# A multi-query attention and MLP block: one term of a software exp moved to GpSimd, GpSimd tied to a port order, and another rule for filling TensorE

## The chip, the cores and the metric

The kernel runs on one core of a Trainium2 chip. The metric is the device time of one execution in microseconds (us); the span in a profile is about 1.7 us shorter. Each run also reports the mean clock that TensorE was granted, as a share of full speed. That number matters more here than usual: the same program can take 809 or 880 us, and the clock tells which of the two it was. A run is called slow in the results when it lies over 1.5% above the fastest run of the same kernel. I compare runs by their clock.

## The reference, cut to what matters

```python
# S = 2048 tokens, D = 640, H = 32 heads of Dh = 20, one shared k and v; F = 1536
q = (xn @ wq) -> [H, S, Dh];  k = xn @ wk;  v = xn @ wv
scores = einsum("bhqd,bkd->bhqk", q, k) * Dh ** -0.5
o = einsum("bhqk,bkd->bhqd", softmax(scores), v)
out = x + o @ wo + (relu(xn @ w1 + b1) ** 2) @ w2 + b2      # xn = layernorm(x)
```

The scores are 32 x 2048 x 2048 numbers, and each needs an exp. The kernel cuts them into 2048 tiles of 128 keys x 512 queries. Everything else is small beside that. Below, "scores" is the first product, and "PV" the second, of the exps with v.

## The kernel before

The kernel is a Python list scheduler. It holds a model of the engines (a duration for each operation, semaphore latencies), places every operation in the model's time, and emits one fixed order for each engine. So the number of exp steps, of tiles given to VectorE and of filling matmuls is fixed when the kernel is built. When I speak below of "the schedule's own time" I mean this layout; it says what was planned, and nothing about how long the chip takes.

A block is 4 heads x 512 queries (32 blocks); for each of 16 key tiles it needs four score tiles. Most score tiles go to ScalarE, two to a step. Four at a time ("a set") go to VectorE, which makes an approximate exp out of bits. These are the parts that the change touches:

```python
ACT_BANKS = ((0, 1), (2, 3))      # PSUM banks of the tiles for ScalarE
DBANKS = (4, 5, 7); DPAIR = (4, 5); PVB = 6      # banks for VectorE's tiles; the PV accumulator
UTIL = 0.66
...
# an exp step on ScalarE: two tiles, 1024 columns
e.activation(out=PT[:, s0:s0 + n, :], in_=ps[:, b0:b0 + n, :], func=AF.Exp, bias=-EXP_SHIFT, scale=SCALE)
...
# a set on VectorE: scores to 16-bit patterns L (D1), two maskings (W, U), two products (T1, T2)
d1.parts = [lambda e: e.tensor_scalar(out=lbuf[a][:, cs].bitcast(U16), in0=src, scalar1=XA, scalar2=XB, op0=ALU.mult, op1=ALU.add)]
W:  tensor_scalar(W, L, 0xFF80, 124,    bitwise_and, bitwise_or)          # VectorE, 2048 columns
U:  tensor_scalar(UU, L, 0x7F, 0x3F80,  bitwise_and, bitwise_or)          # VectorE
T1: tensor_tensor(T, L, UU, mult)                                          # VectorE
T2: tensor_tensor(T, T, UU, mult)      # every other set on GpSimd in two pieces, else VectorE
# exp = L*v + W*(0.5 v) + T*(0.164 v): three PV products for each set, in that order
...
def commit(op):                         # the model lets VectorE and GpSimd run "lock" operations only in turn
    s = start_of(op, op.ready())        # (they share an SBUF port); on the chip nothing enforces it
    ...
def pe_use(t):                          # busy TIME of TensorE in the last 3.4 us
    ...
# before an operation that TensorE would have to wait for:
while pick[0] > free["PE"] + 0.1 + ... and pe_use(...) < UTIL:
    in_pv = pv_blk[0] < NBLK and pv_blk[0] in pv_begun
    fb = [x for x in DBANKS if ...free...]
    if not in_pv and not fb: break
    # a "fill": four matmuls with zero weights into the PV bank or a free score bank
    f_ = Op("fill", "PE", 0.215, [mm(ps[32*jj:32*jj+32, bk, :], zeros32[:, :], kT[:, 0:512], ...) for jj in range(4)], ...)
```

The score matmuls have only 20 rows (Dh) of the array's 128 and the full 128 columns. PV, the MLP and the output use all 128 rows, in four column strips at once.

The softmax here doesn't subtract the row's maximum and nothing guards it: scores larger than these inputs give would overflow.

## Time and profile before

| what | value | view |
|---|---|---|
| runs at the start | 879.42, 824.65, 808.65 us | the runs |
| profiled run | span 868.8 us, clock 0.916 | the cores |
| exp steps on ScalarE | 828 (1656 tiles); 98 sets (392 tiles) on VectorE | groups of instructions |
| ScalarE, 100 to 400 us | busy 298.34 of 300 us, 323 steps, so 0.924 us a step | windows |
| the same, 600 to 720 us | busy 76.83 of 120 us, 75 steps, clock 0.50 | windows |

These are lines of the page of the kernel before. The first is the span, the second the busy time of each engine; in the two others each digit is a fortieth of the span (21.7 us), in tenths.

```profile
span 868.8 us, 22692 instructions
PE 850.7 (98%) x10258; PEld 244.7 (28%) x10258; DVE 683.1 (79%) x998; ACT 786.4 (91%) x845; POOL 319.3 (37%) x211
...
ACT  6799999999999999999899999996666668999995
PEclk9999999999999999999799999995555557999999
```

TensorE's 98% is no use as a measure: ends of matmuls are modelled in the profile, and its row stays at 9 even where the clock halves. ScalarE's row is the one to read. After the start-up it stands at 9 (once at 8) except where the clock row falls to 5, and there it falls to 6. So two things bound this kernel: ScalarE's exp steps, and a TensorE clock that sometimes halves, so that the score matmuls come too late for ScalarE.

The windows view of the kernel before shows the two states side by side (columns: the stretch, its length, busy us and instructions of each engine, clock, DMA share, GB/s):

```profile
core 0: us, PE busy (x) PEld busy (x) DVE busy (x) ACT busy (x) POOL busy (x), PEclk, DMA share, GB/s
100.00:400.00 300.00, 295.29 (x3684) 83.24 (x3685) 261.04 (x363) 298.34 (x323) 123.70 (x76) 1.00 0.02 6
600.00:720.00 120.00, 120.00 (x937) 25.39 (x935) 61.06 (x86) 76.83 (x75) 26.49 (x14) 0.50 0.01 4
```

Next, groups of instructions of the kernel before by line and shape: count, then busy us and the mean ns of one, then the idle time before them and what ended it. L634 is the exp step, L768 the conversion to bits (single and two-bank), L774 W (one of its two groups), L776 U, L778 T1, L785 and L783 the second product T2 on VectorE and on GpSimd.

```profile
L634 ACT ACTIVATE PT<-ps 128x1024 bf16<-128x1024 f32 x828 | 778.2, 1059 | 65.1 <-PE ps L291 62.5
L768 DVE TENSOR_SCALAR x_sb<-ps 128x512 uint16<-128x512 f32 x326 | 218.6, 682 | 107.5 <-PE ps L291 107.0
L783 POOL TENSOR_TENSOR dextra<-dextra 128x1024 bf16<-128x1024 bf16 x98 | 207.5, 2130 | 337.8 <-DVE dextra L778 337.8
L778 DVE TENSOR_TENSOR dextra<-x_sb,dextra 128x2048 bf16<-128x2048 bf16 x98 | 118.5, 1209 | 0.0
L776 DVE TENSOR_SCALAR dextra<-x_sb 128x2048 uint16<-128x2048 uint16 x98 | 75.8, 774 | 0.0
L785 DVE TENSOR_TENSOR dextra<-dextra 128x2048 bf16<-128x2048 bf16 x49 | 59.3, 1211 | 0.0
L774 DVE TENSOR_SCALAR x_sb<-x_sb 128x2048 uint16<-128x2048 uint16 x66 | 45.4, 688 | 0.1
L768 DVE TENSOR_SCALAR x_sb<-ps 128x1024 uint16<-128x1024 f32 x33 | 40.2, 1219 | 18.3 <-PE ps L291 18.2
```

Added up, one set costs VectorE 2.64 (conversion, 258.8/98) + 0.69 (W) + 0.77 (U) + 1.21 (T1) + 0.61 (T2 on half of the sets) = 5.92 us. It takes two steps, 1.85 us, off ScalarE.

**Where the clock halves.** "TensorE: Matmul & The Clock Gate" (the Trainium skill), Part 1, states that a monitor looks at TensorE's activity in free-running windows of 3413 ns and grants half or full clock (1.2 or 2.4 GHz). The trace agrees on window and states: the two low stretches last 10.24 us and 136.5 us, which are 3 and 40 windows, and the clock is 0.5 in them. This is the timeline of TensorE just before the first of them, which begins at 415.5 us (columns: start, length, then what ran):

```profile
411.64 0.62 PE L291 MATMUL ps<-kT,zeros 128*32 128x512 bf16 x8
412.24 0.39 PE L291 MATMUL ps<-qT,kT 20*128 20x512 bf16 x3
412.56 0.40 PE L291 MATMUL ps<-PT,vx 128*32 128x512 bf16 x4
413.15 0.39 PE L291 MATMUL ps<-qT,kT 20*128 20x512 bf16 x2 [0.20 <-ACT PT L634]
414.07 0.39 PE L291 MATMUL ps<-qT,kT 20*128 20x512 bf16 x2 [0.53 <-ACT PT L634]
414.39 0.40 PE L291 MATMUL ps<-PT,vx 128*32 128x512 bf16 x4
```

It is the border between two blocks. The one PV bank is being read out, no fill (`kT,zeros`) is placed, and for 1.4 us (412.97 to 414.39) only score matmuls run, which use 20 rows of 128.

I therefore weighted every matmul of the trace by its **array share**: rows/128 times columns/128, for as long as its moving columns take at the granted clock. (At 2.4 GHz 512 columns are 0.213 us; groups of four strips start 0.22 us apart in the full-clock timeline, for instance 414.39, 414.61, 414.83.) Averaged over the chip's own windows, whose phase is known from the drops (the moments at which the clock falls to half), the two windows before the drops have 0.351 and 0.374. No other window at full clock between 45 us and the last matmul is as low (the next holds 0.378); the mean is about 0.55. This weighting is mine, worked out from the trace; it is no view of the profile.

**The shared port.** "SBUF — State Buffer", "Who interferes with whom", states that VectorE in its two-port modes and GpSimd share a pair of SBUF ports and that whoever comes first blocks the other for the whole instruction. The trace agrees: here W (L774), 0.69 us otherwise, took 1.33 us because GpSimd's square (L457) had begun 0.27 us earlier, and it ended 0.55 us after the square did, a little less than a whole W.

```profile
117.97 1.04 POOL L457 TENSOR_TENSOR big<-hT_tmp 128x512 bf16<-128x512 bf16 x1
118.24 1.33 DVE L774 TENSOR_SCALAR dextra<-x_sb 128x2048 uint16<-128x2048 uint16 x1
```

Over the whole kernel before, such stretching was small: about 9 us of VectorE, nearly all in U (98 times 0.77 - 0.69).

### The profile page before, as it was taken

Reading aid. Unit: us, or ns where it says so; the run is one execution under the profiler, and the core shown is the slowest. Engines: PE = TensorE matmul, PEld = TensorE weight load, DVE = VectorE, ACT = ScalarE, POOL = GpSimd, SP = SyncE. Lnnn points to the kernel's source line nnn. Section 1 sums busy time; section 2 is a strip of 40 time slices with the busy share of each in tenths; the row PEclk is TensorE's granted clock in tenths of the full one; section 3 lists DMA queues with packets and bytes.
Section 4 is the critical chain, followed back from the end, with each engine's and each line's share of the span. In section 5 each row is a group of like instructions: output and inputs, shape, how many; then the busy total and the mean of one; then the engine's idle time right before and its main releaser. Section 6 shows DMA issues by size and latency. Waiting matters only on the chain.

```text
span 868.8 us, 22692 instructions
## 1 busy us (share of the span) xinstructions
PE 850.7 (98%) x10258; PEld 244.7 (28%) x10258; DVE 683.1 (79%) x998; ACT 786.4 (91%) x845; POOL 319.3 (37%) x211
## 2 busy tenths in 40 slices
PE   8999999999999999999999999999999999999997
PEld 3322222222233233222233333221112222322333
DVE  7688888989888888889779887886455457988893
ACT  6799999999999999999899999996666668999995
POOL 5244355452423242534433424444122212342421
PEclk9999999999999999999799999995555557999999
DMA  9300000000000000000000000000000000000000
GB/s 323 90 2 2 2 2 2 2 2 2 2 17 2 17 17 2 16 2 2 2 17 2 17 17 17 2 2 1 1 1 2 16 2 16 17 17 2 2 2 32
DMA packets 11715, 14.94 MB, mean 17 GB/s; under 512 B 2017, under 2 KB 10978, under 8 KB 11618
## 3 DMA queue, kind: packets, MB, share of 16 engines
q1 hardware_dynamic: 10306, 13.44, 4.9%
q8 instruction: 80, 1.31, 0.6%
q10 hardware_dynamic: 1312, 0.05, 0.1%
q14 instruction: 17, 0.14, 0.1%
HBM read 10.87 MB, written 2.62 MB: 16 GB/s over the span
## 4 chain that ended last, share of the span: by engine, by line
PE 62%; ACT 36%; DMA 1%; DVE 1%; issue 0%; SPq 0%; DVEq 0%
PE ps L291 62%; ACT PT L634 35%; DMA x_sb<-in_A_x_dram 1%; DVE out_sb L980 0%; PE ps L403 0%; ACT PT L327 0%; ACT PT L324 0%; DVE Tn L680 0%; ACT xnT L376 0%; SPq L214 0%; DVE T L682 0%; ACT qT L431 0%; PE ps L902 0%; DVE w_sb L529 0%; DVEq L130 0%
## 5 line engine op out<-in xcount | busy, mean ns | idle before, releaser
L634 ACT ACTIVATE PT<-ps 128x1024 bf16<-128x1024 f32 x828 | 778.2, 1059 | 65.1 <-PE ps L291 62.5
L291 PE MATMUL ps<-qT,kT 20*128 20x512 bf16 x2048 | 367.9, 409 | 10.6 <-ACT PT L634 8.2
L768 DVE TENSOR_SCALAR x_sb<-ps 128x512 uint16<-128x512 f32 (+1 forms) x359 | 258.2, 731 | 125.8 <-PE ps L291 125.2
L783 POOL TENSOR_TENSOR dextra<-dextra 128x1024 bf16<-128x1024 bf16 x98 | 207.5, 2130 | 337.8 <-DVE dextra L778 337.8
L291 PEld LDWEIGHTS ps<-qT,kT 20*128 20x128 bf16 x2048 | 82.8, 92 | 340.8 <-ACT PT L634 253.7
L291 PE MATMUL ps<-PT,vx 128*32 128x512 bf16 x1656 | 175.0, 413 | 0.5 <-ACT PT L634 0.5
L778 DVE TENSOR_TENSOR dextra<-x_sb,dextra 128x2048 bf16<-128x2048 bf16 x98 | 118.5, 1209 | 0.0
L291 PE MATMUL ps<-w_sb,big 128*32 128x320 bf16 x1536 | 88.6, 322 | 0.0
L682 POOL TENSOR_TENSOR T<-Tn 128x512 bf16<-128x512 f32 x31 | 43.3, 1397 | 116.7 <-DVE Tn L681 116.7
L291 PE MATMUL ps<-xnT,w_sb 128*32 128x512 bf16 x960 | 81.1, 397 | 0.0
L776 DVE TENSOR_SCALAR dextra<-x_sb 128x2048 uint16<-128x2048 uint16 x98 | 75.8, 774 | 0.0
L291 PE MATMUL ps<-kT,zeros 128*32 128x512 bf16 x816 | 75.3, 414 | 0.0
L291 PEld LDWEIGHTS ps<-PT,vx 128*32 128x32 bf16 x1656 | 42.8, 94 | 108.4 <-issue 103.4
L457 POOL TENSOR_TENSOR big<-hT_tmp 128x512 bf16<-128x512 bf16 x48 | 54.2, 1134 | 51.0 <-DVE hT_tmp L449 50.9
L291 PE MATMUL ps<-wo_pad,OTn 128*32 128x320 bf16 x1024 | 60.6, 322 | 0.8 <-DVE w_sb L529 0.8
L785 DVE TENSOR_TENSOR dextra<-dextra 128x2048 bf16<-128x2048 bf16 x49 | 59.3, 1211 | 0.0
L291 PE MATMUL ps<-xnT,wq_sb 128*20 128x512 bf16 x640 | 57.8, 417 | 0.0
L291 PEld LDWEIGHTS ps<-w_sb,big 128*32 128x32 bf16 x1536 | 36.7, 99 | 33.4 <-issue 21.2
L774 DVE TENSOR_SCALAR x_sb<-x_sb 128x2048 uint16<-128x2048 uint16 x66 | 45.4, 688 | 0.1
L291 PE MATMUL ps<-x_sb,vx 128*32 128x512 bf16 x392 | 40.9, 407 | 0.2 <-DVE Tn L680 0.2
L291 PE MATMUL ps<-dextra,vxc 128*32 128x512 bf16 x392 | 41.1, 409 | 0.0
L680 DVE STREAM_TRANSPOSE Tn<-ps 128x512 f32<-128x512 f32 x32 | 22.9, 714 | 23.2 <-PE ps L291 23.1
(70 smaller groups left out, 386.3 us busy)
## 6 DMA issues: line engine op xcount, KB each, us to landing
w_sb<-in_B_w_dram SPq DMA_DIRECT2D x2, 1920.0 KB, 16.4
xr<-in_A_x_dram SPq DMA_DIRECT2D x16, 160.0 KB, 2.3
out_dram<-out_sb SPq DMA_DIRECT2D x16, 160.0 KB, 1.8
x_sb<-in_A_x_dram SPq DMA_DIRECT2D x3, 640.0 KB, 8.7
wq_sb<-in_A_wq_dram SPq DMA_DIRECT2D x1, 800.0 KB, 7.4
wo_pad<-in_A_wo_dram SPq DMA_DIRECT2D x4, 200.0 KB
x_sb<-in_A_x_dram SPq DMA_DIRECT2D x2, 320.0 KB, 3.8
wk_c<-in_A_wk_dram ACTq DMA_DIRECT2D x1, 25.0 KB, 3.5
```

What stands on the lines that cost most here:

```text
L291: return lambda e: e.matmul(out_, l, r, start=start, stop=stop, tile_position=tp)
L457: sq = q(Op(f"SQ{qc}_{f}", "POOL", 1.2, [lambda e: e.tensor_tensor(out=h2T[:, qc % 2, f, :], in0=hT_tmp[:, k % 2, :], in1=hT_tmp[:, k % 2, ...
L634: return Op(f"ACT{st_['j']}", "ACT", 0.064 + 0.4267 * n, [lambda e: e.activation(out=PT[:, s0:s0 + n, :], in_=ps[:, b0:b0 + n, :], func=AF ...
L680: tn = Op(f"TN{b}", "DVE", 0.72, [lambda e: e.transpose(out=Tn[:, a, :], in_=ps[:, PVB, :])], [lastpv, tm_op.get(b - 2)])
L682: tm = Op(f"TM{b}", *(("POOL", 1.3) if b in TM_POOL else ("DVE", 0.69)), [lambda e: e.tensor_tensor(out=T2[:, a, :].rearrange("p (c d) -> ...
L768: d1.parts = [lambda e: e.tensor_scalar(out=lbuf[a][:, cs].bitcast(U16), in0=src, scalar1=XA, scalar2=XB, op0=ALU.mult, op1=ALU.add)]
L774: s["wop"] = [dv(f"W{n}", 0.74, lambda e: e.tensor_scalar(out=W.bitcast(U16), in0=L.bitcast(U16), scalar1=0xFF80, scalar2=124, op0=ALU.bit ...
L776: s["uop"] = dv(f"U{n}", 0.74, lambda e: e.tensor_scalar(out=UU.bitcast(U16), in0=L.bitcast(U16), scalar1=0x7F, scalar2=0x3F80, op0=ALU.bi ...
L778: s["t1"] = [dv(f"T1_{n}", 1.235, lambda e: e.tensor_tensor(out=T, in0=L, in1=UU, op=ALU.mult), [s["uop"]] + ([("pv", old, 2)] if old else ...
L783: s["t2"].append(dv(f"T2_{n}", 2.15, lambda e, ks=ks: e.tensor_tensor(out=T[:, ks], in0=T[:, ks], in1=UU[:, ks], op=ALU.mult), s["t1"], 4, ...
L785: s["t2"].append(dv(f"T2_{n}", 1.235, lambda e: e.tensor_tensor(out=T, in0=T, in1=UU, op=ALU.mult), s["t1"], P_T))
```

## The change

Its intent, in four parts:

1. The approximate exp is made of other terms: 2**e (W), L*u (T) and a shifted pattern S, the bits of L plus 32. S replaces the second product. GpSimd makes it for every set, straight from L, in two pieces.
2. GpSimd waits for the VectorE operation that precedes it in the model's port order.
3. VectorE's conversions may take any two neighbouring banks (before: banks 4 and 5 only); the PV bank moves to 7.
4. Fills are asked for by array share (0.54 over 3.4 us and 0.4 over 1.7 us) instead of by busy time (0.66), and may be added onto a score tile that waits for ScalarE, when there is no other bank.

The diff holds one thing more: the three PV products of a set may now be issued in any order, each as soon as its term is ready.

The core of the diff (cut; the renaming of buffers and the bookkeeping of PV terms are left out):

```diff
-DBANKS = (4, 5, 7); DPAIR = (4, 5); PVB = 6
+DBANKS = (4, 5, 6); PVBS = (7,); MERGE = 2
-T2POOL = (0, 1)
+SPOOL = (1,)
-UTIL = 0.66
+UTIL = ((3.4, 0.54), (1.7, 0.4))
...
+    def cells(self):
+        if self.name.startswith("QK"):
+            return 0.156 * len(self.parts) * self.dur
+        if self.name.startswith("DQK"):
+            return 0.156 * 0.215
+        return self.dur * (0.625 if self.name.startswith(("QT", "KT")) else 1.0)
...
             if op.lock:
                 lock_free[0] = op.fin
+                if op.eng == "DVE":
+                    lock_dve[0] = op
+                elif lock_dve[0] is not None:
+                    op.deps.append(lock_dve[0])
...
-  W: (L & 0xFF80) | 124 ; U: (L & 0x7F) | 0x3F80 ; T1: T = L*UU
-  T2: T = T*UU on GpSimd (two pieces, 2.15 in the model) for every other set, else on VectorE
+  W:  X & 0xFF80       ; U: T = (X & 0x7F) | 0x3F80 ; T = X*T
+  S on GpSimd, two pieces, 1.06 in the model:
+     e.tensor_scalar(out=M[:, ks].bitcast(U16), in0=X[:, ks].bitcast(U16),
+                     scalar1=float(XS), scalar2=1.0, op0=ALU.add, op1=ALU.mult)
...
+  sa = steps[act_next] if ... and steps[act_next]["qk"].fin is not None else None
+  if not in_pv and not fb and sa is not None and free["PE"] + 0.1 + 0.215 + 0.2 <= free["ACT"]:
+      bk = sa["banks"][len(sa["tiles"]) - 1]
+      f_ = Op("fill", ... mm(ps[32*jj:32*jj+32, bk, :], zeros32[:, :], kT[:, 0:512], False, ...) ...)
+      sa["fill"].append(f_)          # and the exp step then waits for the fill
```

## The prediction

> **What bounds the kernel.** ScalarE's exp, 828 steps of two score tiles. In the windows view, 100 to 400 us, ScalarE is busy 298.3 of 300 us with 323 steps, 0.924 us a step; VectorE 87%. The other 392 of 2048 tiles (98 sets of four) go to VectorE's approximate exp. Each set moved there takes two steps, 1.85 us, off ScalarE.
>
> The second bound is the clock. The profiled run (868.8 us) has the TensorE clock at 0.5 from 415 to 426 us and from 589 to 726 us. From 600 to 720 us there are 75 steps instead of about 130. All lost steps come to about 60 us, so an unthrottled run should be near 809 us; the fastest run is 808.65. So 824.65 and 879.42 are throttle. "TensorE: Matmul & The Clock Gate", Part 1, says that activity in a window of 3413 ns sets a half or full clock; this trace agrees: both low stretches are whole multiples (10.24 and 136.5 us). Weighting each matmul in the trace by the share of the array it uses, the windows just before the drops have 0.35 and 0.37, the lowest since the start-up; the mean is about 0.55. By busy time alone, start-up windows were lower without a drop. Score matmuls use 20 of 128 rows, so they count little: that is why filling by busy time missed them.
>
> **What the change does, per set on VectorE** (durations by line and form): scores to bits 2.6 us, W 0.69, U 0.69 (mean 0.77 with stretching), T1 1.21, and T2 1.21 on half the sets: 5.9 us. T2 leaves VectorE. More one-instruction pairs of score banks are allowed: 1.22 instead of twice 0.68. New: about 5.2 us, 12% less. GpSimd's share is two pieces a set. Its two-input multiply (2.13 us for 1024) can't price a one-input pass; memsets of 512 and 5120 columns (0.53, 4.36 us) give 0.85 us per 1024 plus some start, so an estimate is 1.0 to 1.1 us, 2.1 us a set, the present average: GpSimd stays near 40%.
>
> Port order: when U collided with a GpSimd multiply it took 1.5 to 2.6 us instead of 0.69; "SBUF — State Buffer", on the shared port pair, says that one blocks the other. All stretching sums to about 9 us of VectorE: a set or two.
>
> At the same VectorE share, sets rise from 98 to about 108: some 20 fewer exp steps, 18 to 20 us, all on the critical path while ScalarE stays at 99%.
>
> Fill: new weighting asks 0.54 over 3.4 us, well above 0.37, and score tiles serve as target at block borders, where both drops began. I expect 150 to 200 more four-matmul fills (204 now) and no drops: clock above 0.98.
>
> **Time.** About 789 us median, range 777 to 803. All runs within 1%. Against the median before, 4% faster; against its fast run, 2.4%.
>
> **Shown right by:** ScalarE steps 805 to 812, GpSimd's new line near 1.06 us, no line on VectorE for a second product, U's mean back to 0.69, clock row all 9, low-activity windows gone.
>
> **Wrong if:** the 16-bit integer pass on GpSimd costs 2 us or more (port blocked, VectorE stretched); fills delay score matmuls so ScalarE waits; a border window is still unfilled and the clock drops (15 to 60 us); VectorE waits for score banks, so the sets gained are few.
>
> Faster by over 2%: 0.77; within 2%: 0.18; slower: 0.05.

## The result

| | before | changed |
|---|---|---|
| runs (us) | 808.65, 811.07, 824.65, 879.42 | 791.27, 791.40, 791.44, 791.50 |
| median | 817.86 | 791.42 |
| clock | 0.916 in the profiled run | 0.999 to 1.000 in all four |
| exp steps / sets on VectorE | 828 / 98 | 810 / 107 |
| fills (four matmuls each) | 204 | 195 |

The ratio of the fast runs is 0.9772, 95% interval 0.9747 to 0.9797: faster. Ratios in this document are the mean time of one kernel's fast runs over that of the other's of the same rounds, so 0.9772 is not quite the ratio of the medians above (0.968, which also counts throttled runs of before).

The same lines of the page of the changed kernel:

```profile
span 789.7 us, 22849 instructions
PE 776.8 (98%) x10294; PEld 238.3 (30%) x10294; DVE 662.8 (84%) x981; ACT 761.1 (96%) x827; POOL 319.0 (40%) x327
...
ACT  5899999999999999999999999999999999999994
PEclk9999999999999999999999999999999999999999
```

Groups of the changed kernel: L652 is the exp step, L797 the shifted pattern on GpSimd, L784 the conversions, L792 the product, L790 U, L788 W (one of its two groups).

```profile
L652 ACT ACTIVATE PT<-ps 128x1024 bf16<-128x1024 f32 x810 | 752.9, 1051 | 11.1 <-PE ps L308 8.5
L797 POOL TENSOR_SCALAR dextra<-x_sb 128x1024 uint16<-128x1024 uint16 x214 | 220.7, 1047 | 341.3 <-DVE dextra L790 211.2 <-DVE x_sb L784 112.9 <-DVE x_sb L788 9.8
L784 DVE TENSOR_SCALAR x_sb<-ps 128x512 uint16<-128x512 f32 x300 | 200.4, 682 | 54.0 <-PE ps L308 53.1
L792 DVE TENSOR_TENSOR dextra<-x_sb,dextra 128x2048 bf16<-128x2048 bf16 x107 | 132.7, 1240 | 0.0
L784 DVE TENSOR_SCALAR x_sb<-ps 128x1024 uint16<-128x1024 f32 x64 | 77.6, 1213 | 18.7 <-PE ps L308 18.4
L790 DVE TENSOR_SCALAR dextra<-x_sb 128x2048 uint16<-128x2048 uint16 x107 | 73.2, 685 | 0.0
L788 DVE TENSOR_SCALAR x_sb<-x_sb 128x2048 uint16<-128x2048 uint16 x72 | 50.2, 697 | 0.3
```

And the window from 100 to 400 us:

```profile
100.00:400.00 300.00, 297.86 (x3801) 85.33 (x3797) 259.05 (x365) 298.45 (x323) 129.06 (x126) 1.00 0.02 6
```

What to read: a step of ScalarE still takes 0.924 us (298.45/323), VectorE is as busy as before (259.05 against 261.04 us), and a set now costs it 2.60 + 0.70 + 0.68 + 1.24 = 5.22 us instead of 5.92. The nine sets gained take 18 exp steps away; 18 x 0.924 = 16.6 us, and the unthrottled run of before, 808.65, less 16.6 is 792.0. That is the measured time within 0.6 us; experiments 9 and 10 show that such closeness is partly luck. Part 2 of the gain is the spread: none of the four runs was throttled.

The arithmetic fits, but it does not show which part did what. My theory was: (a) the fast-run gain is exp steps, paid for by the cheap pass on GpSimd; (b) a drop of the clock needs one of the chip's windows with an array share under about 0.375, and the change leaves none; (c) the port order is a detail. The rivals: the new fill rule itself, or the port order, or the two-bank conversions carry the gain; the clock follows busy time and not array share; the steady clock comes from something else.

### The profile page after: what moved, and what is told of

Read it like the earlier page. It is cut to its first block, busy times and chain, and to the rows that moved or that the text cites. A ratio compares the mean times of both kernels' runs of the same rounds, so it can differ in the third digit from the quotient of the medians.

```text
span 789.7 us, 22849 instructions
## 1 busy us (share of the span) xinstructions
PE 776.8 (98%) x10294; PEld 238.3 (30%) x10294; DVE 662.8 (84%) x981; ACT 761.1 (96%) x827; POOL 319.0 (40%) x327
## 4 chain that ended last, share of the span: by engine, by line
PE 72%; ACT 26%; DVE 1%; DMA 1%; issue 0%; SPq 0%; DVEq 0%
PE ps L308 71%; ACT PT L652 25%; DMA x_sb<-in_A_x_dram 1%; DVE Tn L698 0%; DVE out_sb L1009 0%; PE ps L420 0%; ACT PT L344 0%; ACT PT L341 0%; DVE x_sb L784 0%; ACT xnT L393 0%; SPq L226 0%; DVE T L700 0%; ACT qT L448 0%; PE ps L919 0%; DVE w_sb L546 0%
## 5 line engine op out<-in xcount | busy, mean ns | idle before, releaser
L652 ACT ACTIVATE PT<-ps 128x1024 bf16<-128x1024 f32 x810 | 752.9, 1051 | 11.1 <-PE ps L308 8.5
L797 POOL TENSOR_SCALAR dextra<-x_sb 128x1024 uint16<-128x1024 uint16 x214 | 220.7, 1047 | 341.3 <-DVE dextra L790 211.2
L308 PE MATMUL ps<-qT,kT 20*128 20x512 bf16 x2048 | 335.6, 384 | 5.1 <-ACT PT L652 3.9
L784 DVE TENSOR_SCALAR x_sb<-ps 128x512 uint16<-128x512 f32 (+1 forms) x364 | 277.4, 775 | 72.7 <-PE ps L308 71.5
L308 PE MATMUL ps<-PT,vx 128*32 128x512 bf16 x1620 | 161.7, 389 | 0.3 <-ACT PT L652 0.2
L792 DVE TENSOR_TENSOR dextra<-x_sb,dextra 128x2048 bf16<-128x2048 bf16 x107 | 132.7, 1240 | 0.0
L790 DVE TENSOR_SCALAR dextra<-x_sb 128x2048 uint16<-128x2048 uint16 x107 | 73.2, 685 | 0.0
L700 POOL TENSOR_TENSOR T<-Tn 128x512 bf16<-128x512 f32 x31 | 34.3, 1107 | 42.2 <-DVE Tn L699 16.1
L788 DVE TENSOR_SCALAR x_sb<-x_sb 128x2048 uint16<-128x2048 uint16 x72 | 50.2, 697 | 0.3
L308 PE MATMUL ps<-dextra,vxt 128*32 128x512 bf16 x428 | 42.0, 383 | 0.0
L308 PE MATMUL ps<-dextra,vxs 128*32 128x512 bf16 x428 | 41.7, 383 | 0.0
L466 DVE TENSOR_SCALAR hT_tmp<-ps,b1col 128x512 bf16<-128x512 f32 x48 | 35.3, 736 | 6.4 <-PE ps L308 6.3
```

What stands on the lines that cost most here:

```text
L308: return lambda e: e.matmul(out_, l, r, start=start, stop=stop, tile_position=tp)
L466: o = q(Op(f"RL{qc}_{f}", "DVE", 0.75, [lambda e: e.tensor_scalar(out=hT_tmp[:, k % 2, :], in0=ps[:, bk, :], scalar1=b1col[:, f:f + 1], sc ...
L652: return Op(f"ACT{st_['j']}", "ACT", 0.064 + 0.4267 * n, [lambda e: e.activation(out=PT[:, s0:s0 + n, :], in_=ps[:, b0:b0 + n, :], func=AF ...
L700: tm = Op(f"TM{b}", *(("POOL", 1.1) if b in TM_POOL else ("DVE", 0.69)), [lambda e: e.tensor_tensor(out=T2[:, a, :].rearrange("p (c d) -> ...
L788: s["w"] = [dv(f"W{n}", 0.74, lambda e: e.tensor_scalar(out=W.bitcast(U16), in0=X.bitcast(U16), scalar1=0xFF80, scalar2=None, op0=ALU.bitw ...
L790: s["u"] = [dv(f"U{n}", 0.74, lambda e: e.tensor_scalar(out=T.bitcast(U16), in0=X.bitcast(U16), scalar1=0x7F, scalar2=0x3F80, op0=ALU.bitw ...
```

## The experiments

Twelve kernels ran, all with correct results, each beside runs of the kernel before on the same chip. Before any ran I had their counts of steps and fills from the scheduler, and the "low windows": the total time of starting points, in the schedule's own time, from which a 3.4 us window would hold under 0.375 of the array. The 0.375 is my cutoff, set just above the 0.374 of the trace before.

### 1. The fill rule alone, on the kernel before (b_fill)

```diff
 kernel before
-UTIL = 0.66, busy time of the last 3.4 us
+UTIL = ((3.4, 0.54), (1.7, 0.4)) of the array share; score tiles allowed as fill target (as in the change)
```

> The kernel before with only the new fill rule (array-weighted use, 0.54 over 3.4 us and 0.4 over 1.7 us, score tiles allowed as target): still 98 sets, 828 exp steps, 251 fills instead of 204. Theory (the fast-run gain is exp steps, the fill only removes the throttle): clock 1.0 in all five runs, spread under 1%, time 808 to 814 us, no gain on the fast run of before. Rival (the fill is where the fast-run gain comes from): below 800 us.

Measured: 826.56, 860.27, 940.88, 970.94, 1029.83 and 1029.83 us, clock 0.983 down to 0.751. **A miss.** The kernel got 251 fills instead of 204 and was throttled in every run; its median is 955.91 us, against 814.76 for the kernel before beside it. The clock row of its page (profiled run, 858.5 us):

```profile
PEclk9999999999999855556999999999999999999999
```

The long drop (31 windows, from 296 us) came after a window of 0.344; a second one, at 678 us, lasted a single window. So the rule does not make the windows that it asks for. It can only place a fill where TensorE would otherwise wait and where a bank is free; in this kernel the schedule's own time still held 3.2 us of low windows (before: 2.8), and in the trace 5.2 us. I had read "asks for 0.54" as "gets 0.54".

### 2. The old fill rule on the changed kernel (a_oldfill)

```diff
 changed kernel
-pe_use: array share over 3.4 and 1.7 us; score tiles allowed
+pe_use: busy time over 3.4 us, 0.66; no score tiles
```

> The changed kernel with the fill rule of before (busy time 0.66 over 3.4 us, no score tile as target): the schedule comes out at 106 sets, 812 steps, 164 fills. Theory: the fastest run is 792 to 796 us, and at least one of five runs loses over 8 us with a clock under 0.99. Rival (fill is the gain): fastest run over 800 us. Rival (the new stage pattern keeps the clock by itself): all five within 1% at clock 1.0.

Measured: 794.07, 794.10, 801.30, 801.51, 803.19, 860.81 us, the first two at clock 0.999, the others at 0.987 (three) and 0.908. As the theory had it: without a drop 812 steps give 794 us, so the fast-run gain does not need the new fill rule; the steady clock does.

### 3. Same fills, same length, fewer rows (a_fill20), and no fills (a_nofill)

```diff
 changed kernel, a_fill20
-mm(ps[...], zeros32[:, :],    kT[:, 0:512],    ...)
+mm(ps[...], zeros32[0:20, :], kT[0:20, 0:512], ...)     # both kinds of fill
 changed kernel, a_nofill
-... and pe_use(...) < 1.0:
+... and False:
```

> The changed kernel, same schedule and same 195 fills of the same length, but every filling matmul multiplies 20 rows instead of 128. Busy time of TensorE is unchanged; array-weighted use falls by 0.84 of the fills, and in the trace of the changed kernel about 24 windows of 3.4 us would then lie below 0.375. Theory (the clock follows the share of the array used): clock below 0.95 in every run, time over 815 us. Rival (the clock follows busy time): clock 1.0, 791 us as before.

> The changed kernel with no fills at all once the exp steps have begun; 107 sets, 810 steps. Theory: about 34 windows below 0.375, so the clock is at half for a large part of the span, slower than with the 20-row fills or like it: over 820 us. Rival (fills cost more in queueing than the throttle does): below 791 us.

Measured: a_fill20 1155.81 to 1221.29 us at clock 0.587 to 0.632; a_nofill 1004.34 to 1048.38 us at 0.678 to 0.715. The clock row of a_fill20:

```profile
PEclk9885955555555555599865559995555555775556
```

Its fills occupy TensorE as long as before, and the windows before its drops had busy shares up to 0.73, yet the clock fell. (Busy share here is the part of a window in which at least one matmul streams its columns.) Fills of 20 rows are worse than none: they take TensorE's time and count for almost nothing. They also cost a little more than the full ones, which a learner should know before calling the two equal: a group starts 0.33 us after a 20-row fill, and 0.23 us after a full one. How much of the extra time is due to which is not shown. **The clock follows the share of the array's rows in use, not busy time.** Columns were not varied alone: the score matmuls use all 128, and the others come as four strips side by side.

Over the nine traces that have drops before their end (so that the phase of the windows is known; 6 of the 38 drops lie in the start-up), all 38 windows just before a drop held 0.374 or less by my weighting. Of some 1500 other windows at full clock, all without a drop after them, 13 held less than 0.375 too; so by my weighting every drop followed a low window, but the edge is not exact. By busy share the two kinds overlap entirely: up to 0.73 before a drop, down to 0.44 without one.

Two recounts of the same traces support the weights. If the 20-row fills are counted as full ones, as time would count them, the windows before drops hold up to 0.58, and two thirds of the other windows hold no more than that. If the score matmuls are weighted by 0.08 or 0.25 instead of 20/128 = 0.156, 21 or 26 other windows hold no more than the highest before a drop, instead of 13.

### 4. The kernel before with a heavier fill target (b_fill66)

```diff
 b_fill
-UTIL = ((3.4, 0.54), (1.7, 0.4))
+UTIL = ((3.4, 0.66), (1.7, 0.6))
```

> The kernel before with the new fill rule asking more (0.66 over 3.4 us, 0.6 over 1.7 us). Laid out in the schedule's own time, stretches in which a 3.4 us window would start and hold under 0.375 of the array add up to 0.6 us, against 3.2 us in b_fill and 2.8 us in the kernel before. Still 98 sets, 828 exp steps, 327 fills. Theory (a drop needs a window under 0.375 at the chip's free-running phase; the exp steps set the rest): at least four of six runs at clock over 0.995 and at 808 to 813 us. Rival (the old formula keeps the clock down whatever the fills): most runs over 820 us as in b_fill. Rival (a steady clock alone gives the gain of the change): under 800 us.

Measured: 818.86, 818.86, 818.93, 818.95, 819.44, 823.13 us; clock 0.999 to 1.000 in five, 0.992 in the profiled run, whose one drop fell into the start-up, at 20 us. The clock came out as foreseen: the old formula keeps full clock once its schedule has no low windows. A steady clock alone does not give the gain. The time missed my range by 6 us: with 327 fills the kernel is 10 us slower than the undisturbed kernel before, with the same 828 steps. From 100 to 400 us its ScalarE made 319 steps instead of 323:

```profile
100.00:400.00 300.00, 298.78 (x3878) 85.21 (x3870) 256.76 (x362) 297.68 (x319) 128.82 (x77) 1.00 0.02 6
```

Sets and steps are the same, so the added fills are the likely price; through which wait was not looked at.

### 5. The shifted pattern on VectorE (a_sdve50)

```diff
 changed kernel
-SPOOL = (1,)
+SPOOL = (0,)
-UTIL = ((3.4, 0.54), (1.7, 0.4))
+UTIL = ((3.4, 0.54), (1.7, 0.5))     # chosen because its schedule keeps only 0.2 us of low windows
```

> The changed kernel with the shifted pattern made by VectorE (one pass of about 0.69 us a set) instead of GpSimd, fill target 0.54 and 0.5 so that the schedule keeps only 0.2 us of low windows: 96 sets, 832 exp steps. Theory (the gain is work taken off VectorE, hence exp steps): clock about 1.0 in most runs, 22 steps more than the change at 0.92 us, 809 to 814 us. Rival (the new three-term form or the banks give the gain, not GpSimd): under 800 us.

Measured: 811.64 to 812.01 us in six runs, all at clock 1.000; ratio to before 1.0005 (0.9967 to 1.0043). The whole fast-run gain is gone (the undisturbed runs of before beside it took 809 us). 832 steps are 22 more than in the change, 22 x 0.924 = 20.3 us; 791.4 + 20.3 = 811.7. Here is the pattern's line on VectorE; 0.686 us a set is all it takes there, and it costs 11 sets.

```profile
L799 DVE TENSOR_SCALAR dextra<-x_sb 128x2048 uint16<-128x2048 uint16 x96 | 65.8, 686 | 0.0
```

So the new three-term form and the freer banks gain nothing by themselves here. What gains is that GpSimd can make the third term for every set: it needs only one input and does not wait for the product. The edit also brings 277 fills instead of 195; the sum of steps leaves no time for them, so its exactness is partly luck.

### 6. No score tiles as fill target (a_noscore)

```diff
 changed kernel
-sa = steps[act_next] if act_next < len(steps) and steps[act_next]["qk"].fin is not None else None
+sa = None
```

> The changed kernel without score tiles as fill target: 187 fills instead of 195, 107 sets, 810 steps. In the schedule's own time the low windows rise from 0 to 6.4 us, about two hits per run. Theory: nearly every run loses time to a half clock, median over 800 us; the fastest, if any run is spared, 791 to 794 us. Rival (five fills of 0.2 us cannot matter): six runs within 1% at 791 to 794 us.

Measured: 792.80, 794.10, 794.18, 795.75, 802.63, 839.39 us with clocks 1.000, 0.998, 0.998, 0.995, 0.984, 0.934. Five of six runs had a drop, but most were one window long; the median, 794.96 us, is under the 800 that I had given. In the change only 5 of the 195 fills go onto score tiles. They close holes for which the scheduler found no other bank. This is such a place in the changed kernel, where the scheduler had put one (its list places them at 146.5, 217.1, 284.1, 561.2 and 698.8 of its own time, which runs about 1.5 us ahead of the chip here):

```profile
217.61 0.39 PE L308 MATMUL ps<-qT,kT 20*128 20x512 bf16 x2
218.29 0.39 PE L308 MATMUL ps<-qT,kT 20*128 20x512 bf16 x2 [0.29 <-ACT PT L652]
218.60 0.40 PE L308 MATMUL ps<-kT,zeros 128*32 128x512 bf16 x4
218.83 0.39 PE L308 MATMUL ps<-PT,vx 128*32 128x512 bf16 x4
```

Beside the border of the kernel before above: there two pairs of score matmuls followed one another with only waits between them; here a fill follows the second pair.

### 7. Without the port order (a_noport), and the port order alone on the kernel before (b_port)

```diff
 changed kernel, a_noport
-                elif lock_dve[0] is not None:
-                    op.deps.append(lock_dve[0])
 kernel before, b_port: the same lines added
```

> The changed kernel without the wait that holds GpSimd to the modelled order; schedule, sets and steps unchanged (107, 810). Theory: the shifted pattern is ready at the moment VectorE wants W and U, so without the wait GpSimd takes the shared port in front of U or T and VectorE loses up to 1 us a set: W, U and T lines longer by over 60 us in sum, 800 to 850 us. Rival, as in my prediction: worth a set or two, 791 to 796 us.

> The kernel before with only the wait that holds GpSimd to the modelled port order; schedule unchanged (98 sets, 828 steps, 204 fills). Theory (the order matters where GpSimd's piece becomes ready together with VectorE's masking passes, which is new in the change; before, the second multiply came only after the first): U's mean falls from 0.77 to 0.69 us, the fastest run stays at 806 to 810 us, and some runs are still slowed by the clock. Rival (the port order is worth as much to the kernel before as to the changed one): fastest run under 800 us, or all runs at clock 1.0.

Measured, b_port: 808.37, 808.44, 810.59, 823.40, 823.50, 849.40, 872.36 us; same as before (ratio 0.9953, 0.9885 to 1.0020). U's mean fell to 0.69 us, but the sets are fixed in the schedule, so nothing came of it.

Measured, a_noport: 901.27 to 1020.54 us, median 961.06, clock 0.752 to 0.880. This is far beyond both expectations. Its groups of instructions (L786 W, L788 U, L795 the shifted pattern):

```profile
L795 POOL TENSOR_SCALAR dextra<-x_sb 128x1024 uint16<-128x1024 uint16 x214 | 279.6, 1321 | 374.3 <-DVE x_sb L782 374.3
L788 DVE TENSOR_SCALAR dextra<-x_sb 128x2048 uint16<-128x2048 uint16 x107 | 117.0, 1093 | 0.0
L786 DVE TENSOR_SCALAR x_sb<-x_sb 128x2048 uint16<-128x2048 uint16 x72 | 71.9, 999 | 0.3
```

(W has a second group of 35, 38.5 us.)

The windows view of this kernel, first a stretch at full clock, then one at half clock:

```profile
100.00:300.00 200.00, 195.35 (x2459) 56.16 (x2461) 184.71 (x240) 195.53 (x211) 99.77 (x81) 1.00 0.02 5
320.00:480.00 160.00, 160.00 (x1171) 30.31 (x1163) 92.08 (x112) 101.10 (x99) 56.17 (x42) 0.50 0.02 5
```

The first of these stretches in the changed kernel:

```profile
100.00:300.00 200.00, 198.48 (x2510) 56.51 (x2510) 173.15 (x246) 198.88 (x215) 83.90 (x82) 1.00 0.02 5
```

The pattern now starts when the last conversion ends (released by L782), the moment at which VectorE wants W and U. W and U together take 227.4 us instead of 147.7, 80 us of stretching; I had expected over 60. This is one collision in its timeline: GpSimd's two pieces come in at 212.95, and U and the next W take 1.5 us each.

```profile
212.79 0.68 DVE L786 TENSOR_SCALAR x_sb<-x_sb 128x2048 uint16<-128x2048 uint16 x1
212.95 2.86 POOL L795 TENSOR_SCALAR dextra<-x_sb 128x1024 uint16<-128x1024 uint16 x2 [1.24 <-DVE x_sb L782]
213.39 1.53 DVE L788 TENSOR_SCALAR dextra<-x_sb 128x2048 uint16<-128x2048 uint16 x1
214.84 1.52 DVE L786 TENSOR_SCALAR dextra<-x_sb 128x2048 uint16<-128x2048 uint16 x1
```

At full clock that costs little: 211 steps instead of 215 in 200 us, 2%. But its trace holds 11.8 us of low windows instead of 0.02. The likely reason is that TensorE, which runs in a fixed order, now waits for VectorE where the schedule had it working. The clock is at half for 338 us (two stretches of 167.3 and 170.7 us). In 160 us of it (320 to 480 us) ScalarE made 99 steps where 173 fit, 68 us lost; over 338 us that is an estimate of 144 us. With 2% of 791 us, 16 us, the sum is 951 us; the profiled run took 950.57. So, by this estimate, most of the damage goes by way of the clock. The order matters for this layout; a layout planned without it was not tried.

### 8. GpSimd's pass with one operation (a_s1op)

```diff
 changed kernel
-scalar1=float(XS), scalar2=1.0, op0=ALU.add, op1=ALU.mult), list(sdep), 4
+scalar1=float(XS), scalar2=None, op0=ALU.add), list(sdep), 4
```

> The changed kernel with the idle second operation (times 1.0) taken off GpSimd's pass; same result, same schedule. In the trace of before a GpSimd pass with one operation took 0.53 us for 128 columns and one with two operations 0.19 us for 4, so an estimate for 1024 columns is 2.5 to 3 us if the one-operation form is slower for each element. Theory (the second operation is there because the form with one is slow): pieces of 2 us or more, VectorE's passes stretched, over 830 us. Rival (the form makes no difference): 1.05 us and 791 us.

Measured: 1235.43 to 1282.44 us, clock 0.584 to 0.621. Its line for the pass:

```profile
L797 POOL TENSOR_SCALAR dextra<-x_sb 128x1024 uint16<-128x1024 uint16 x214 | 597.5, 2807 | 424.0 <-DVE dextra L790 256.1 <-DVE x_sb L784 152.7 <-DVE x_sb L788 11.2
```

2.81 us instead of 1.05 for the same 1024 columns, because a multiplication by 1.0 was left out. With that form the changed kernel takes half as long again as the kernel before (ratio 1.52). "GPSIMD Engine Reference", section 4.1, calls one-input work there "roughly line-rate"; section 3.1 gives about 1.03 cycles an element for simple loops. The pass with two operations comes near it (1047 ns for 1024 elements at the 1.2 GHz of that section is 1.2 cycles with its start); the pass with one takes 3.3 and does not. Why, no run shows.

### 9. Single conversions only (a_merge1)

```diff
 changed kernel
-MERGE = 2
+MERGE = 1
```

> The changed kernel without two-bank conversions: 424 single ones instead of 300 singles and 64 pairs, 106 sets, 812 steps; low windows in the schedule's time 0.9 us. Theory (pairs are worth one set): fastest run 792 to 796 us. Rival (the pairs carry much of the saving): over 800 us at clock 1.0.

Measured: 797.64, 797.91, 798.88 us and 804.84 at clock 0.986 (the others at 0.997 to 1.000; the 0.997 is one window at half clock in the start-up). Between the two expectations. The two-bank conversions are worth 6 us: 2 steps (1.8 us), and some 4 us more that the count of steps does not explain.

### 10. Another layout without low windows (a_layout)

```diff
 changed kernel: six constants of the scheduler
-DLEAD = 13.0, CLOSE = 2, MERGE = 2, RIDE = 0.1, D1LAT = 0.4,  UTIL = ((3.4, 0.54), (1.7, 0.4))
+DLEAD = 10.0, CLOSE = 1, MERGE = 3, RIDE = 0.15, D1LAT = 0.35, UTIL = ((3.4, 0.56), (1.7, 0.42))
```

> The changed kernel laid out anew by six constants of its scheduler, picked only because the new layout has no window of 3.4 us under 0.375 in the schedule's own time (lowest 0.39); 108 sets, 808 steps, 199 fills. Theory (any layout without low windows keeps the clock; the steps set the rest): all six runs at clock 0.999 or more, spread under 0.5%, 788 to 793 us. Rival (the layout of the change is special, or the low windows are not the cause): some runs lose over 5 us with a clock under 0.99.

Measured: 799.96, 800.39, 800.50, 800.52, 801.76, 808.01 us; clock 0.997 to 1.000 in five, 0.987 in the last. **A miss on the time**, and two runs (0.997 and 0.987) are more disturbed than the 0.999 that I had given. They have no trace; the start-up (12 to 45 us) holds some low windows in every layout, the changed kernel's too, so drops there are possible, but I can't show it.

The 9 us are at full clock and with two steps fewer. A count in the traces gives a possible cause: TensorE goes into row-tiled score matmuls 841 times in this kernel for its 808 steps (33 more than steps), in the changed kernel 818 times for 810 (8 more). A score matmul for VectorE that does not ride along with an exp step's pair makes a trip of its own, like the single one at 104.57 us here:

```profile
104.24 0.40 PE L308 MATMUL ps<-PT,vx 128*32 128x512 bf16 x4
104.57 0.39 PE L308 MATMUL ps<-qT,kT 20*128 20x512 bf16 x1
104.89 0.40 PE L308 MATMUL ps<-dextra,vxs 128*32 128x512 bf16 x4
105.22 0.39 PE L308 MATMUL ps<-qT,kT 20*128 20x512 bf16 x3
```

Every change between the two kinds starts 0.32 us after the one before, where like groups start 0.22 us apart. 25 trips more at an estimated 0.32 us each are 8 us. I have not tested that, and it can't be the whole story: a_merge1 makes only 823 trips (11 more than its 812 steps) and b_fill66 as many as it has steps (828), yet they too are slower than their steps say, by 4 and 10 us. So layouts of nearly the same step count differ by up to 10 us at full clock for reasons that stay open, and a sum of steps that fits within 1 us has had some luck.

### All kernels by their low windows

The low windows of each trace (from 45 us on, at full clock only), divided by 3.413 us, give the number of low windows that one run should meet, as its phase is arbitrary. Beside it, how many runs had a clock under 0.99:

| kernel | low windows in the trace, us | expected hits a run | runs under 0.99 |
|---|---|---|---|
| changed | 0.02 | 0.01 | 0 of 4 |
| a_layout | 0.08 | 0.02 | 1 of 6 |
| a_sdve50 | 0.30 | 0.09 | 0 of 6 |
| b_fill66 | 0.50 | 0.15 | 0 of 6 |
| a_merge1 | 0.80 | 0.23 | 1 of 4 |
| a_oldfill | 2.59 | 0.76 | 4 of 6 |
| before | 3.77 | 1.10 | 24 of 44 |
| b_port | 4.18 | 1.23 | 4 of 7 |
| b_fill | 5.15 | 1.51 | 6 of 6 |
| a_noscore | 5.47 | 1.60 | 2 of 6 (5 under 0.999) |
| a_noport | 11.8 | 3.46 | 6 of 6 |

Each row rests on one trace, and the cutoff of 0.375 comes from these traces. a_fill20, a_s1op and a_nofill are left out: 21 to 28 us by the same count, and every run under 0.72.

This fits the spread of the kernel before, too. Its 44 runs beside the experiments lie at 809, 811 to 812, 816, 824 and 850 us again and again, as if a few places were hit or missed as the phase of the windows falls, each with its own price. In its one trace there are eight such places, six of them at block borders; which place gives which time was not traced.

## Why the prediction was right, point by point

- **Time: right.** 789 predicted, 791.42 measured, in the range. Faster by over 2% in the fast runs (0.9772).
- **Steps, and the price of a set: right.** 805 to 812 steps predicted, 810 measured; 5.2 us a set predicted, 5.22 measured; GpSimd at 40%. a_sdve50 shows that without GpSimd's pass the fast-run gain is gone: put back on VectorE it gives 811.9 us. That the times agree to about 1 us is partly luck, since a_layout, with two steps fewer, is 9 us slower.
- **GpSimd's pass: right (1.05 us), for a reason that I did not know.** I had priced a one-input pass from memsets. a_s1op shows that the ordinary form takes 2.81 us, which would have put the time where "wrong if" says.
- **Fills: the step that failed.** "150 to 200 more four-matmul fills": there were 9 fewer (195). And "the new weighting asks 0.54, well above 0.37 ... and no drops" took the target for the result. b_fill has the weighting, 251 fills, and throttles in every run; the changed kernel keeps the clock with fewer fills. What counts is that its layout has no low window. The outcome, clock 1.0 in all runs, was right; the means was not.
- **Clock by array share, threshold near 0.37: right**, shown by a_fill20 and by 38 drops out of 38 (two of which it was read from). It is an edge that every drop lies under and not a rule that makes one: 13 lower windows had no drop.
- **Port order: mis-sized.** "Worth a set or two." To the kernel before it is worth nothing (b_port, 808.4 us), to the changed kernel's layout it is worth most of all: without it the fastest run takes 901 us and the median 961, 170 us more. I priced the collisions that the old kernel had. The change makes new ones, since the new pass becomes ready together with W and U, and I did not price what they do to the clock.
- **U back to 0.69 us: right**, with a small remainder moved to the product: T's mean is 1.240 us, 3.3 us in all above T1's 1.209 before (up to 1.88 us for one).
- **Two-bank conversions:** counted by me within VectorE's set; a_merge1 makes them worth 6 us, of which 4 stay open.

## What to carry to other kernels

When an engine looks idle enough to take over work, ask what it collides with at the moment that its new work becomes ready, and hold it to an order if the layout depends on that order: the collision may be cheap in itself and dear in what it sets off. Where a clock gate watches activity, find the weakest window of the layout and not the mean, weight matmuls by the rows that they use, and price a filling rule by what it could place. And measure the exact form of an instruction before you plan with it: one idle operation more made this one 2.7 times as fast.

## What the Trainium skill lacked or had wrong

- "TensorE: Matmul & The Clock Gate", Part 1, says that the clock follows how busy TensorE was and warns of idle gaps over about 3.4 us. In these runs it followed the share of the array's rows in use: the clock fell after windows that were 73% busy and stayed after windows that were 44% busy; every one of 38 drops followed a window with an array share of 0.374 or less (13 others as low had none), and fills of 20 rows instead of 128 took the changed kernel from clock 1.0 to 0.63.
- The same page gives the way back to full clock as one busy window. Here low stretches lasted up to 351.6 us (a_fill20) while TensorE worked on, and windows with a share of up to 0.74 at half clock did not end them, while others with 0.54 were the last of theirs. What ends them stays open.
- "GPSIMD Engine Reference", section 4.1: one-input elementwise work is "roughly line-rate". On 1024 16-bit elements the two-operation form took 1.05 us, the one-operation form 2.81 us. The page does not tell them apart.
- "SBUF — State Buffer", "Who interferes with whom", agrees (W 1.33 us behind a square of 1.04 us). It could add the price of the second effect: 80 us of stretching became about 160 us of time, an estimated 144 of them by way of the clock.
- "TensorEngine Tiling (Array Packing)", "Key Properties", says that a change of tiling mode drains TensorE, but no page gives its cost; here, between row-tiled and column-tiled matmuls, such a change started 0.32 us after the group before, and like groups 0.22 us apart.
